# MoE matmuls as pairs in two 64-row tiles, with two score groups and wide evacuations, in a fused attention and MoE kernel

## The chip, the cores and the metric

The kernel runs on one core of one Trainium2 chip. The metric is the device time in microseconds (us), the median of five runs. Engines: PE is TensorE (matmuls; PEld are its weight loads), DVE is VectorE, ACT is ScalarE, POOL is GpSimd, SP is SyncE, which here only issues DMAs. Matmul results land in PSUM: eight banks, each of 128 partitions x 512 float32. A matmul may use the whole array (128 rows of the contraction) or a part of it as a "tile"; two matmuls in the tiles of rows 0-63 and 64-127 can run abreast.

## The reference

```python
# attention with pooled queries: B, H, S, D = 8, 8, 1152, 64; factor 2
q_pool = q.reshape(B, H, S // 2, 2, D).mean(axis=3)          # 576 queries per head
scores = matmul(q_pool, k.T) / sqrt(D)
attn   = softmax(scores)
x      = matmul(attn, v)     # -> (B * 576, H * D) = (4608 tokens, 512)
# MoE layer with a maximum of two branches, d_ff = 1024
h1, h2 = x @ w1, x @ w2
out    = maximum(h1, h2) @ w_out                             # (4608, 512) float32
```

The kernel works in bfloat16 with float32 accumulation. It uses max(h1, h2) = relu(h1 - h2) + h2: with wd = w1 - w2 and w21 = w2 @ w_out, both made once on the chip, out = relu(x @ wd) @ w_out + x @ w21.

## The kernel before

**Work on TensorE.** The 64 heads are taken as 32 pairs. For each pair:

- *Scores* (`scores`, L480-506): keys and pooled queries lie transposed, head 0 in partitions 0-63, head 1 in 64-127. A score group is 512 score columns for both heads: two matmuls abreast in the two 64-row tiles, each into its own bank of a two-bank tensor `sps`. There are 324 groups over the whole run, about 10 per pair. ScalarE then does one exp over both banks (1024 columns), from `sps` into `et`. A group may be overwritten when its exp is done.
- *AV* (`av_jobs`, L399-454): exp(scores) times V with a column of ones for the sum. It comes as two jobs, one per head: three units of nine 128-row matmuls of 65 columns each, and in the first job a unit of 18 column-tiled matmuls for the last 64 queries (the "rest", L427). VectorE then divides into `xnat`.
- *Transposes* bring `xnat` into `xT`, by DMA on SP's queue or, for the first and last batch, by TensorE.

MoE jobs use `xT`. An *h job* (`h_jobs`, L632) makes 128 rows of relu(x @ wd) for up to 512 tokens with four 128-row matmuls; VectorE applies the maximum with zero into the buffer `gT`. A *p job* (`p_job`, L657) makes the output of 128 tokens with twelve 128-row, 512-column matmuls (four with `w21`, eight with `wo`); VectorE copies it into one of four output slots `osb`, from which it is stored. After the last score group ScalarE takes half of these evacuations.

**Banks.** Three score groups take six banks (`sps0` to `sps2`); two banks, `fb0` and `fb1`, are lanes for jobs, one job to a bank. After the last score group the six banks become lanes too (`more_banks`).

**Order.** All instructions are put in order in Python before the program is built. `Plan` keeps for each engine the time at which it is free, with a cost per operation, a latency to other engines and 0.1 us when TensorE changes its tile shape (a unit's `mode`: "f" 128 rows, "s" 64 rows, "c" column tiles). The loop at L991 takes the next piece of TensorE work: a burst of two score groups (three once the attention of a first batch is done) when they can start without a stall, else a unit of a job whose inputs are ready, by rank. On the chip each engine runs its instructions in this fixed order and waits on semaphores. Loads of q, k, v (SP), casts (POOL) and DMA transposes (SP) are put in by due times of the same plan (`flush`, L804).

The lines that carry the order and the lanes:

```python
for g in range(3):                       # more_banks, after the last group
    ...
r = g % 3                                # scores: ring of three groups
...
done = [b for b in range(B) if all(av_half.get(b * NHP + j) == 2 for j in range(NHP))]
return 3 if done else 2                  # burst_size
...
if ready and stall <= 0.1:               # main loop
    emit_burst(ready)
elif fresh:
    emit_unit(min(fresh, key=lambda c: c[1:])[3])
```

Of the kernel before, what the change touches and what calls it, by code (L numbers as in the profile page):

```python
# [15 lines left out]
class Plan:  # L16
# [28 lines left out]

    def when(self, eng, r=(), w=(), after=()):

        if any(k not in self.writer for k in r):
            return 1e9
        t = self.free.get(eng, 0.0)  # L50
        for d in self.deps(r, w, after)[0]:
            p = self.ops[d]
            if p["eng"] != eng or p["dma"] is not None:
                t = max(t, p["seen"] + 0.05)
        return t

    def op(self, eng, fn, r=(), w=(), dma=None, cost=0.1, mode="f", after=(), solo=False):
        n = len(self.ops)
# [6 lines left out]
        self.last[eng] = n  # L65
        t = self.when(eng, r, w, after)
        if dma is not None:
# [5 lines left out]
        else:  # L73
            if eng == "PE" and mode != self.mode:
# [4 lines left out]
        self.ops.append(dict(eng=eng, fn=fn, deps=deps, raw=raw, dma=dma, w=tuple(w),  # L79
                             seen=seen, end=self.free[eng], solo=solo))  # L80
        for k in r:
# [6 lines left out]
    def solve(self):  # L88
# [3 lines left out]
        for n, o in enumerate(ops):  # L92
# [3 lines left out]
            for d in sorted(o["deps"], reverse=True):  # L96
                p = ops[d]
                if p["dma"] is None:
                    if p["eng"] == eng and (eng == "PE" or eng != "DVE" and d not in o["raw"]):
                        continue  # L100
                    key = p["eng"]
                else:
                    key = ("dma", p["dma"])
                if kn.get(key, -1) >= d:
                    continue
                o["waits"].append(d)
                for k, v in p["know"].items():
                    if kn.get(k, -1) < v:
                        kn[k] = v
                kn[key] = max(kn.get(key, -1), d)  # L110
# [39 lines left out]
class Job:  # L150


    def __init__(self, kind, units, evac, done=None, nb=None):
        self.kind, self.units, self.evac, self.done = kind, units, evac, done
        self.nb = nb


def bass_funnel_attn__then__act_maxout2_kernel(
# [32 lines left out]
    with ctx:  # L191
# [33 lines left out]
        gT = g16.rearrange("p (f n) -> p f n", f=NF)  # L225
        osb = [stage[:, NC_ * F + s * E:NC_ * F + (s + 1) * E] for s in range(4)]

        sps = [psum([P, 2, 512], f"sps{g}") for g in range(3)]
        fb = [psum([P, 512], f"fb{g}") for g in range(2)]
        fb += [sps[g][:, half, :] for g in range(3) for half in range(2)]  # L230

# [244 lines left out]
        def skeys(g):  # L476
            return [key for i, t, *_ in pieces(g) for key in (f"kT{i % 3}.{t}", f"qpT{i % 3}")] + (
                ["qpT0.0"] if g == 0 else [])

        def scores(g):  # L480
            r = g % 3

# [133 lines left out]
        ocount = [0]  # L616
        held = {}

        def store(lo, s, c0=0, c1=E, engs=("SP", "SP")):
# [12 lines left out]
        def h_jobs(nb, tail):  # L632
# [4 lines left out]
            for ft in range(NF):  # L637
# [16 lines left out]
                jobs.append(Job("h", [part(ct) for ct in range(NC_)], evac, nb=nb))  # L654
            return jobs

        def p_job(lo, tail, c0=0, c1=E):  # L657
# [75 lines left out]
        X_PE = (0, B - 1)  # L733
        DEPTH = 4.0
        LAG = 600
        Q_PE = 5
# [99 lines left out]

        def more_banks():

            for g in range(3):
                for half in range(2):  # L840
                    m = 2 + 2 * g + half
                    lane[m] = None
                    plan.writer[f"f{m}"] = plan.writer[f"s{g}"]
                    plan.readers[f"f{m}"] = set(plan.readers[f"s{g}"])

        def ready_at(job):
            return plan.when("PE", r=job.units[0][0])

        def burst_size():

            done = [b for b in range(B) if all(av_half.get(b * NHP + j) == 2 for j in range(NHP))]
            return 3 if done else 2

        def more_moe():
            tail = nxt == NGR
            while h_at[0] < len(hblocks):
                n0, n1 = hblocks[h_at[0]]
# [3 lines left out]
                if plan.when("PE", r=keys) > now() + (9.0 if tail else 0.0):  # L861
                    break
                queue["h"].extend(h_jobs(h_at[0], tail))
                h_at[0] += 1
            while p_at[0] + P <= h_end[0] and f"w21{NC_ - 1}" in plan.writer:
                if p_at[0] + P < NTOK:
                    queue["p"].append(p_job(p_at[0], tail))
                else:
                    queue["p"].extend(p_job(p_at[0], tail, *c) for c in ((0, 384), (384, E)))
                p_at[0] += P  # L870

        def refill():

            more_moe()
            soon = now() + (0.05 if nxt else 0.3)
            for kind in "qkxa":
                if queue[kind] and (ready_at(queue[kind][0]) <= soon):
                    return queue[kind].pop(0)
            busy = [j.kind for j in lane.values() if j]
            for kind in "wh" if queue["a"] and "p" in busy else "wph":  # L880
                if queue[kind] and ready_at(queue[kind][0]) <= soon:
                    return queue[kind].pop(0)
            if nxt == NGR:
                for kind in "axph":
                    if queue[kind]:
                        return queue[kind].pop(0)
            return None

        def burst_now(size):
# [11 lines left out]
            for g in todo_g:  # L901
                s = plan.when("PE", r=skeys(g), w=[f"s{g % 3}"])
                stall += max(0.0, s - t)
# [3 lines left out]
        def emit_burst(todo_g):  # L907
# [10 lines left out]
            if nxt == NGR:  # L918
                more_banks()
            if queue["q"]:  # L920
                for kk in (0, 1):
                    if lane[kk] is None and plan.when(
                            "PE", r=queue["q"][0].units[0][0], w=[f"f{kk}"]) <= now() + 0.05:
# [4 lines left out]
        def emit_unit(kk):  # L928
# [5 lines left out]
            job.evac(kk)  # L934
            lane[kk] = None
            if job.kind == "a":
                av_half[job.nb] = av_half.get(job.nb, 0) + 1
# [3 lines left out]
            elif job.kind == "h":  # L941
                h_left[job.nb] = h_left.get(job.nb, NF) - 1
                while h_left.get(h_ok[0]) == 0:
                    h_end[0] = hblocks[h_ok[0]][1]
                    h_ok[0] += 1
            elif job.kind == "p":
                p_parts[job.nb] = p_parts.get(job.nb, 0) + 1
                if p_parts[job.nb] == (2 if job.nb == NTOK else 1):
                    p_got.add(job.nb)
# [41 lines left out]
        while p_end[0] < NTOK:  # L991
            flush()
            for kk in sorted(lane, key=lambda kk: plan.when("PE", w=[f"f{kk}"])):
                if lane[kk] is None:
                    lane[kk] = refill()
            cand = []
            for kk in lane:
                job = lane[kk]
                if job is not None:
                    t = plan.when("PE", r=job.units[0][0], w=[f"f{kk}"])  # L1000
                    cand.append((t, -rank[job.kind], len(job.units), kk))
# [5 lines left out]
            if len(turn) < len(fresh) and plan.mode == "f" and nxt < NGR:  # L1007
                fresh = [c for c in fresh if c not in turn]
            ready, stall = burst_now(burst_size())
            if ready and stall <= 0.1:  # L1010
                emit_burst(ready)
# [72 lines left out]
```

## Time and profile before

| | |
|---|---|
| median of 5 runs | 380.22 us (379.67 to 382.66) |
| the profiled execution | 382.66 us; its span, first to last instruction, 380.9 us |
| granted TensorE clock | 1.0 throughout |
| busy: PE / ACT / POOL / DVE | 357.4 / 316.3 / 161.5 / 149.9 us |
| exps (L493) | 336 instructions, 306.2 us, 1008 ns on average |
| scores (L486) | 1152 matmuls, 100.5 us busy |
| AV (L415, L427) | 2304 + 576 matmuls, 81.9 + 15.2 us |
| h matmuls, 128 x 512 into `fb` (L640) | 192, 380 ns each as recorded |
| p matmuls, 128 x 512 into `fb` (L667) | 195 with `wo` and 96 with `w21`, 380 ns each as recorded |
| evacuation of 128 x 512 (L651, L699) | 692 and 691 ns |
| HBM read / written | 62.91 / 9.44 MB |

How to read it: a matmul's recorded duration runs until its last result is in PSUM, while the next one may already stream; so durations of matmuls overlap, and what one costs is seen from the distance between starts. "Idle before" in a group names what released the first instruction after the idle time. In the chain of work, a piece lasts until the next piece starts. "issue" is time in which the profile shows nothing that the engine waited for.

### The profile page before, as it was taken

To read this page: it belongs to the slowest core of one execution; us is meant where nothing else is said; L and a number is where in the kernel's file an instruction comes from. 1 tells how busy PE (TensorE), PEld (TensorE's weight loads), DVE (VectorE), ACT (ScalarE), POOL (GpSimd) and SP (SyncE) were. 2 spreads that over 40 slices of the span, in tenths; PEclk is the share of its full clock that TensorE was granted. 3 is DMA by queue.
4 is the path that set the end of the run, shared out by engine and by line. 5 is a ranking of instruction groups with operands and counts; after the bars stand their busy time and mean duration, and the time that the engine had idled before them with its cause. 6 is when DMAs were issued, how large, how long until landed. Compare 5 with 4: busy or idle time off the path is not lost.

```text
span 380.9 us, 11393 instructions
## 1 busy us (share of the span) xinstructions
PE 357.4 (94%) x4983; PEld 204.7 (54%) x5040; DVE 149.9 (39%) x348; ACT 316.3 (83%) x358; POOL 161.5 (42%) x133
## 2 busy tenths in 40 slices
PE   2889999999999999999998899999999999999995
PEld 1465555555555555555555355555555555566462
DVE  2565774532344233532253133432343324843121
ACT  1999999999999999999988889998999999103120
POOL 1265996667416750675165318570485120000000
PEclk9999999999999999999999999999999999999999
DMA  7999999999899998998999989997999761012323
GB/s 258 408 393 403 398 236 279 254 261 346 179 201 390 214 243 183 388 245 219 233 338 280 113 239 390 235 281 114 325 268 307 110 209 29 2 29 57 83 65 100
DMA packets 93537, 88.58 MB, mean 233 GB/s; under 512 B 66096, under 2 KB 66352, under 8 KB 93488
## 3 DMA queue, kind: packets, MB, share of 16 engines
q1 hardware_dynamic: 92448, 86.28, 85.8%
q10 hardware_dynamic: 1040, 1.57, 1.1%
q8 instruction: 39, 0.64, 0.7%
q14 instruction: 10, 0.08, 0.1%
HBM read 62.91 MB, written 9.44 MB: 190 GB/s over the span
## 4 chain that ended last, share of the span: by engine, by line
PE 77%; ACT 16%; issue 2%; DMA 2%; DVE 1%; another core or an unknown queue 0%; SPq 0%; ACTq 0%
PE sps L486 18%; PE fb L667 18%; PE fb L415 17%; ACT et L493 16%; PE fb L640 12%; PE sps L667 5%; PE fb L427 3%; PE sps L640 3%; DMA kraw<-in_k_dram 2%; PE fb L606 1%; DVE xnat L447 0%; DVE xnat L442 0%; PE fb L383 0%; PE fb L548 0%
## 5 line engine op out<-in xcount | busy, mean ns | idle before, releaser
L493 ACT ACTIVATE et<-sps 128x1024 bf16<-128x1024 f32 (+1 forms) x336 | 306.2, 1008 | 10.7 <-PE sps L486 8.5
L314 POOL TENSOR_TENSOR qp<-qraw 64x576 bf16<-64x576 f32 x60 | 85.1, 1419 | 54.4 <-DMA qraw<-in_q_dram 47.0
L486 PE MATMUL sps<-qpT,kT 64*128 64x512 bf16 (+7 forms) x1152 | 100.5, 290 | 5.9 <-issue 3.0
L415 PE MATMUL fb<-vE,et 128*128 128x65 bf16 x2304 | 81.9, 193 | 1.2 <-DVE xnat L447 0.5
L415 PEld LDWEIGHTS fb<-vE,et 128*128 128x128 bf16 x2304 | 74.3, 97 | 11.4 <-DVE xnat L447 4.3
L486 PEld LDWEIGHTS sps<-qpT,kT 64*128 64x128 bf16 x1152 | 40.1, 95 | 65.8 <-ACT et L493 33.3
L321 POOL TENSOR_SCALAR vE<-vraw 128x1152 bf16<-128x1152 f32 x32 | 37.8, 1182 | 67.1 <-DMA vraw<-in_v_dram 66.8
L651 DVE TENSOR_SCALAR stage<-fb 128x512 bf16<-128x512 f32 (+3 forms) x62 | 40.1, 646 | 53.9 <-PE fb L640 48.3
L640 PE MATMUL fb<-xT,wd 128*128 128x512 bf16 (+3 forms) x268 | 57.0, 346 | 2.1 <-issue 1.4
L667 PE MATMUL fb<-wo,stage 128*128 128x512 bf16 (+1 forms) x203 | 54.0, 377 | 1.3 <-issue 0.3
L279 POOL TENSOR_SCALAR kbf<-kraw 128x1152 bf16<-128x1152 f32 x31 | 37.5, 1209 | 22.3 <-DMA kraw<-in_k_dram 12.5
L437 DVE RECIPROCAL rc<-fb 128x5 f32<-128x5 f32 (+1 forms) x64 | 12.1, 188 | 83.1 <-PE fb L415 83.0
L640 PEld LDWEIGHTS fb<-xT,wd 128*128 128x128 bf16 x284 | 24.4, 98 | 25.7 <-issue 4.5
L699 DVE COPY stage<-fb 128x512 f32<-128x512 f32 x24 | 16.6, 691 | 43.1 <-PE fb L667 39.3
L667 PEld LDWEIGHTS fb<-wo,stage 128*128 128x128 bf16 x224 | 19.5, 98 | 21.0 <-issue 3.3
L447 DVE TENSOR_TENSOR xnat<-fb,rc 128x256 bf16<-128x256 f32 x64 | 27.2, 425 | 2.2
L667 PE MATMUL fb<-w,xT 128*128 128x512 bf16 (+1 forms) x100 | 26.8, 377 | 0.7 <-issue 0.3
L696 ACT COPY stage<-fb 128x512 f32<-128x512 f32 x3 | 1.8, 586 | 20.3 <-PE fb L667 20.3
L427 PEld LDWEIGHTS fb<-vE,et 128*64 128x64 bf16 x576 | 11.6, 111 | 7.9 <-issue 7.6
L667 PE MATMUL sps<-wo,stage 128*128 128x512 bf16 (+1 forms) x70 | 15.8, 361 | 0.1
L667 PEld LDWEIGHTS fb<-w,xT 128*128 128x128 bf16 x112 | 9.9, 98 | 11.0 <-DVE xnat L447 1.1
L427 PE MATMUL fb<-vE,et 128*64 128x65 bf16 x576 | 15.2, 197 | 0.0
(45 smaller groups left out, 136.6 us busy)
## 6 DMA issues: line engine op xcount, KB each, us to landing
kraw<-in_k_dram SPq DMA_DIRECT2D x32, 576.0 KB, 7.5
vraw<-in_v_dram SPq DMA_DIRECT2D x32, 576.0 KB, 7.6
qraw<-in_q_dram SPq DMA_DIRECT2D x31, 576.0 KB, 7.0
out_dram<-stage SPq DMA_DIRECT2D x59, 128.0 KB, 2.6
xT<-in_moe_w_dram SPq DMA_DIRECT2D x4, 512.0 KB, 10.2
stage<-in_moe_w_out_dram SPq DMA_DIRECT2D x4, 512.0 KB, 13.1
stage<-in_moe_w_dram SPq DMA_DIRECT2D x4, 512.0 KB, 12.9
out_dram<-stage ACTq DMA_DIRECT2D x11, 128.0 KB, 2.6
```

Of the source, the lines that this page charges most:

```text
L279: op("POOL", lambda g: g.tensor_scalar(kbf[s][:, :, :, :].rearrange("p t h d -> p h t d"), kraw[r][:, :, :, :], 1.0, 1.0, ALU.mult, ALU.mu ...
L314: op("POOL", lambda g, half=half, a=a: g.tensor_tensor(qp[s][:, :, half, :], a[:, :, 0, :], a[:, :, 1, :], ALU.add), r=[f"qraw{r}"], w=[f" ...
L321: op("POOL", lambda g: g.tensor_scalar(vE[r][:, :, :, 0:D].rearrange("p t h d -> p h t d"), vraw[r][:, :, :, :], 1.0, 1.0, ALU.mult, ALU.m ...
L415: last = e.matmul(fb[m][:, sb * 66:sb * 66 + 65], et[:, a:a + P], vE[vs][:, t, half, 0:65], start=(t == 0), stop=(t == NT - 1))
L427: last = e.matmul(fb[m][rows(half), NCH * 66:NCH * 66 + 65], et[:, a:a + NB], vE[vs][:, t, half, 0:65], start=(t == 0), stop=(t == NT - 1))
L447: dve(lambda e: e.tensor_tensor(xnat[xs][:, 0:NCH, c:c + D], a[:, 0:NCH, 0:D], rc[half][:, 0:NCH].unsqueeze(2).to_broadcast([P, NCH, D]), ...
L486: last = e.matmul(sps[r][:, h, col:col + hi - lo], kT[i % 3][rows(h), t, :], qpT[i % 3][rows(h), lo:hi], start=True, stop=True)
L493: op("ACT", lambda e: e.activation(et2[:, :, c:c + z - a], sps[r][:, :, a - g * W:z - g * W], EXP, scale=scale), r=[f"s{r}"], w=keys + [f" ...
L640: return e.matmul(fb[m][:, 0:size], wd[:, ct, ft * P:(ft + 1) * P], xT[:, ct, n0:n1], start=(ct == 0), stop=(ct == NC_ - 1))
L651: dve(lambda e: e.tensor_scalar_max(gT[:, ft, g0:g0 + size], fb[m][:, 0:size], 0.0), [f"f{m}"], w, 0.16 + size / 960.0)
L667: return e.matmul(fb[m][:, 0:c1 - c0], lhs, rhs[:, c0:c1], start=(j == 0), stop=(j == NC_ + NF - 1))
L699: dve(lambda e: e.tensor_copy(osb[o][:, :], fb[m][:, :]), [f"f{m}"], [f"osb{o}", f"f{m}"], 0.69)
```

## The change

1. **Duos.** While score groups are left, MoE work comes as pairs of jobs: two h jobs (two blocks of 128 rows of wd's output, same tokens), or two p jobs (two blocks of 128 tokens). Each 128-row contraction is cut into two of 64 rows. In the first half of a duo job, job k = 0 uses array rows 0-63 and job k = 1 rows 64-127; in the second half they swap. Each unit issues two matmuls, one per tile, into the two banks of one two-bank tensor. Their tile shape is that of the scores. At the swap a `fence` makes TensorE wait for its own last matmul on the same banks.
2. **Banks.** When the first MoE work is queued (and the number of groups done is a multiple of three), the score ring goes from three groups to two, and the third pair of banks becomes a pair of lanes. From then on there are two bank pairs for jobs. Two AV halves of one head pair can be joined in one bank pair.
3. **Wide evacuations.** VectorE evacuates both banks of a duo in one instruction of 1024 columns.
4. **Order.** From then on score bursts are of one group, and the main loop has its own rules: it stays with 128-row work until ScalarE's planned lead falls under `FLOOR` (0.1 us) or no score is ready, and goes to 128-row work from a lead of `LEAD` (1.4 us). A duo job starts only when no other lane has a duo with more than `NEAR` (6) units left.

After the last score group everything is as before: what is left of the MoE work is taken as single 128-row jobs on eight lanes.

```diff
+        wide = [psum([P, 2, 512], "fb")] + sps
+        fb = [w[:, half, :] for w in wide for half in range(2)]
...
+        def ring(g):
+            return g % 3 if g < turn_at[0] else (g - turn_at[0]) % 2
         def scores(g):
-            r = g % 3
+            r = ring(g)
...
+        def duo(r, cost, pair, turned):
+            def plan_it(m):
+                op("PE", lambda e: pair(e, m), r=r, w=[f"f{m}", f"f{m + 1}"], cost=cost, mode="s",
+                   fence=turned)
+            return r, plan_it, cost, "s", 2 if turned else 0
...
+        def h_pairs(nb):
...
+                    def pair(e, m):
+                        for k in range(2):
+                            z = rows(turn ^ k)
+                            last = e.matmul(
+                                fb[m + k][:, 0:size], wd[z, ct, (f0 + k) * P:(f0 + k + 1) * P],
+                                xT[z, ct, n0:n1], start=(turn == 0 and ct == 0),
+                                stop=(turn == 1 and ct == NC_ - 1))
+                        return last
+                    return duo([f"wd{ct}"] + xkeys(n0, n1), 0.217 * size / 512, pair, turn == 1 and ct == 0)
+                def evac(m, f0=f0):
...
+                    dve(lambda e: e.tensor_scalar_max(
+                        gT[:, f0:f0 + 2, g0:g0 + size], wide[m // 2][:, :, 0:size], 0.0),
...
+        def p_pair(lo):
...
+                def pair(e, m):
+                    for k in range(2):
+                        z = rows(turn ^ k)
+                        n = lo + k * P
+                        if j < NC_:
+                            lhs, rhs = xT[z, j, n:n + P], w21[z, j, :]
+                        else:
+                            c = n % RING
+                            lhs, rhs = gT[z, j - NC_, c:c + P], wo[z, j - NC_, :]
+                        last = e.matmul(fb[m + k][:, :], lhs, rhs, start=(turn == 0 and j == 0),
+                                        stop=(turn == 1 and j == NC_ + NF - 1))
+                    return last
...
+            def evac(m):
+                ocount[0] += ocount[0] % 2
+                o = ocount[0] % 4
+                ocount[0] += 2
+                for s in (o, o + 1):
+                    if s in held:
+                        store(*held.pop(s))
+                dve(lambda e: e.tensor_copy(
+                    osb2[:, o:o + 2, :], wide[m // 2][:, :, :]), [f"f{m}", f"f{m + 1}"],
...
         def burst_size():
+            if turn_at[0] < NGR:
+                return 1
...
         while p_end[0] < NTOK:
             flush()
+            if phase() == 1 and nxt % 3 == 0 and queue["h"]:
+                turn_at[0] = nxt
+                more_banks((2,))
...
             ready, stall = burst_now(burst_size())
+            if phase() == 2:
+                lead = plan.free.get("ACT", 0.0) - now()
+                soft = [c for c in fresh if lane[c[3]].units[0][3] != "s"]
+                firm = [c for c in fresh if c not in soft]
+                if plan.mode != "s" and soft and (not ready or stall > 0.05 or lead > FLOOR or not CUT):
+                    pick = [c for c in soft if lane[c[3]].units[0][3] == plan.mode] or soft
+                    emit_unit(min(pick, key=lambda c: c[1:])[3])
+                    continue
+                if ready and stall <= (0.005 if firm and lead >= 0.6 else 0.05):
+                    emit_burst(ready)
+                    continue
+                if soft and (lead >= LEAD or not firm or (ready is None and nxt < NGR)):
+                    emit_unit(min(soft, key=lambda c: c[1:])[3])
+                    continue
+                if firm:
+                    emit_unit(min(firm, key=lambda c: c[1:])[3])
+                    continue
```

## The prediction

> **What bounds the kernel now.** I read the page first (busy times, slices, groups), then the sums over stretches of 20 us, then the chain in order of time, then a few microseconds of the timeline. Page, parts 1 and 2:
>
> ```profile
> PE 357.4 (94%) x4983; PEld 204.7 (54%) x5040; DVE 149.9 (39%) x348; ACT 316.3 (83%) x358; POOL 161.5 (42%) x133
> ...
> ACT  1999999999999999999988889998999999103120
> ...
> PEclk9999999999999999999999999999999999999999
> ```
>
> Two engines are full at once: ScalarE until about 325 us, then hardly used; TensorE to the end, at full clock. The stretches (columns: PE, PEld, DVE, ACT, POOL busy, then clock, DMA) split the run into three parts:
>
> ```profile
> 40.00:60.00 20.00, 18.66 (x324) 11.08 (x326) 14.38 (x25) 19.91 (x24) 17.72 (x12) 1.00 1.06 279
> ...
> 80.00:100.00 20.00, 19.71 (x277) 10.60 (x277) 5.05 (x14) 19.74 (x22) 13.99 (x11) 1.00 1.13 285
> ...
> 200.00:220.00 20.00, 16.93 (x206) 9.01 (x209) 5.64 (x13) 17.08 (x20) 9.04 (x7) 1.00 0.98 192
> ...
> 340.00:360.00 20.00, 19.89 (x136) 11.67 (x136) 5.56 (x13) 3.81 (x10) 0.00 (x0) 1.00 0.26 69
> ```
>
> Up to 64.5 us there is no MoE work (start). From 64.5 to 322 us scores, exps, attention-times-V (AV) and MoE share TensorE (joint part). From 322 to 381 us TensorE works off the MoE that is left (tail, 59 us). The chain gives TensorE's prices, since its pieces run on to the start of the next one:
>
> ```profile
> 78.70 2.01 PE fb L415 x63
> ...
> 87.32 0.40 PE fb L427 x18
> 87.73 1.19 PE fb L415 x36
> ...
> 93.04 2.05 PE fb L667 x9
> 95.08 0.86 PE sps L486 x12
> 95.95 2.05 PE fb L667 x9
> ...
> 141.79 1.40 PE fb L667 x6
> ...
> 201.63 1.53 issue
> ...
> 211.00 1.17 issue
> ```
>
> (2.05 - 1.40)/3 = 0.217 us per 128-row, 512-column matmul; what is left of the 1.40 is 0.10 us: the gap before a score burst. The AV pieces say the same: (2.01 - 1.19)/27 = 0.0304 us each, 36 of them 1.09 us, 0.10 left; the column-tiled rest of AV (L427) has 0.30 and 0.10. Score matmuls use 64-row tiles, everything around them 128-row tiles. Over all changes of tile shape in this trace the gap beyond the columns has a median of 92 to 99 ns in either direction; I take **0.097 us per switch**. In the score burst 12 matmuls, two abreast, make three groups: 0.86 - 0.10 = 0.76, so a pair of 64-row, 512-column matmuls costs at most 0.25 us; uninterrupted pairs in the trace start 0.216 us apart (0.010 more where a semaphore wait stands between).
>
> The timeline gives the latencies between TensorE and ScalarE:
>
> ```profile
> 212.18 0.82 PE L486 MATMUL sps<-qpT,kT 64*128 64x128 bf16 x11 [1.17 <-issue]
> ...
> 212.60 2.86 ACT L493 ACTIVATE et<-sps 128x1024 bf16<-128x1024 f32 x3 [1.36 <-PE sps L486]
> ```
>
> From a score group's first matmul to its exp: 0.42. Three exps take 2.86 and one alone 1.04 (its group's mean), so exps follow each other every 0.91. A score matmul that waits for an exp starts 0.05 after its end: 1.09 after that exp's start.
>
> **The change, by its parts.** Where planner and pools decide, I counted in the order of the built program.
>
> *Switches.* A MoE duo is in the scores' tile shape, so only AV, transposes and the weight product still switch. Counted over the whole program: 290 changes of shape before, 202 after (joint part 222 to 130). 88 x 0.097 = **-8.5 us** of TensorE. These lie on the path: counted from the first score group after the first MoE matmul to the last, 264 groups come to 57.5, AV to 64.8, MoE to 105.1 and 222 switches to 21.5, together 248.9 of the 257.5 us, so nothing else covers them. The gain shows in the tail: MoE matmuls issued before the last score rise from 491 full-size units to 524 (a duo counts one), 33 x 0.217 = 7.2 us of tail.
>
> *The duo itself.* No trace shows two row tiles accumulating. Nearest row: score pairs, 0.216 us for 512 columns against 0.217 for one 128-row matmul, so 0 per duo. Bounds: 0 (a stream of 512 columns cannot go below a 512-column stream) and 0.217 (the two run one after the other) on each of 524. I take 0, as the scores have both tiles, both banks and the same weight loads.
>
> The number of weight loads doubles. In score bursts four loads of 93 to 96 ns start within 0.02 us while the first pair streams, and the next pair follows when the first has drained, 136 ns after a 320-column pair: hidden. The Trainium skill, "TensorE: Matmul & The Clock Gate", The mechanism (in Part 3), speaks against this: weight loads overlap running matmuls only when the row group differs, and a duo's next loads go to the same two row groups. By that rule each duo would show a load, some 0.095 us x 524 = +50 us; by the row it is 0.
>
> *The turn.* Half-way the tiles swap banks, and a fence makes TensorE wait for its own last matmul. 55 duo jobs are in the order; 38 carry a wait; in 30 of them at least one other duo or score group (0.217) stands between, in 8 nothing. A 512-column matmul is recorded with 0.38 us and its semaphore is seen 0.04 to 0.05 later: 0.43 - 0.217 = 0.21 us lost, 8 x 0.21 = **+1.7**. Lower end 0 (a later wait would have come anyway), upper 38 x 0.21 = 8.
>
> *Two score groups in place of three.* Now a score may not start until the exp two groups back is done, and everything on TensorE's queue stands behind that wait. One head pair worked by hand from its order (0.217 per group or duo, AV column block of 9 matmuls 0.274, the rest 0.30, switch 0.10). Group c starts at 0, the exps of a, b, c at -1.09, -0.18, 0.73. Then rest and three blocks: group d at 0.217 + 0.30 + 0.82 + 3 x 0.10 = 1.64, its exp 0.42 later at 2.06 (ScalarE, done with c at 1.64, is dry for 0.42). Group e at once, 1.86 (free since 0.73 + 1.09 = 1.82), exp 2.97. Five blocks: group f at 1.86 + 0.217 + 1.37 + 2 x 0.10 = 3.65, exp 4.07 (dry 0.19). One duo: g at 4.08 (free at 4.06), exp 4.98. Four duos: h at 5.17 (free at 5.16). From there windows of three duos and a group, 0.87, against exps every 0.91: TensorE waits 0.04 in each of five. Sum 0.2 us a pair. A pair whose second AV run has six blocks gives 0.24, once, where group e must wait. 26 pairs x 0.21 = 5.5 us. Today's waits: 257.5 - 248.9 = 8.6, less 3.5 for late transposes (the two "issue" pieces and a smaller one), less 2.0 for waits passed in a burst (169 x 0.012), less 1 of small gaps: 2.1. So **+3.4**. Ends: 0 and twice the 5.5, +9.
>
> ScalarE's dry spells cost nothing by themselves, since TensorE is busy in them: exps need 262 x 0.91 = 238 us of a joint part of some 258.
>
> *Waits in the stream.* Groups not preceded by a switch: 169 before, about 211 after, 42 x 0.012 = **+0.5**.
>
> *The turning point.* The ring shrinks at a multiple of three groups, and MoE work starts after 61 groups in place of 59 for the same TensorE work (46.6 us). Where ScalarE sets the pace that is up to 2 x 0.91 less 2 x 0.217 = 1.4 later; 0 where it does not. I take the middle, **+0.7**.
>
> *Wide evacuations, the joined AV halves, stores.* A 512-column evacuation takes 692 ns, 256 columns 422: 0.154 + 1.05 ns per column, so 1.23 us for both banks against 1.38. VectorE (39% busy) covers it. Behind the wide copy on VectorE's queue wait AV's reciprocals, up to 0.54 us later than now; a second bank pair with a duo job covers that. If it is busy too, 0.5 on some of 26 pairs, at most +13 x 0.5 = 6. Four output slots remain and the store queue on SP carries the same transfers (63 out against 61, the two taken from ACT's queue). Loads and transposes keep their number; the late ones at 201 and 211 us I leave where they are: 0, between -3.5 (they fall into cover) and +3.5 (twice as much).
>
> Sum: -8.5 + 1.7 + 3.4 + 0.5 + 0.7 = **-2.2 us**. The profiled execution spans 380.9 and took 382.66; the median of the five is 380.22, 2.4 lower, and I put the difference on the median: **378.0**.
>
> **The rivals.**
> - *Full gain* (waits fall where TensorE is late anyway, as ScalarE drifts by hundredths): -8.5 + 1.7 + 0.5 = -6.3, **373.9**. For: the hand-worked pair is late or just in time at half its groups. Against: the three-duo windows are shorter than an exp.
> - *Slower: two groups are too few.* At the scores next to AV and in the three-duo windows TensorE waits on exps far more than 0.21 a pair. Each 0.1 us a pair is 2.6 us; from 0.37 us a pair it is slower by 0.5%. At 0.6 us: -2.2 + 26 x 0.39 = +8, **388**. For: bursts of one leave no group in hand when a transposed operand comes late, and 1.36 us of ScalarE idle at 211 us happened with three. Against: TensorE, not ScalarE, is the fuller one.
> - *Duos do not overlap fully.* 8 ns each give +4.2 and 382.2; one after the other +114. Against: the score pairs.
> - *Nothing to gain* because transfers set the joint part: DMA is at 0.9 to 1.2 of its engines from 20 to 300 us, and four more output tiles are stored in that time. The tail's 7.2 us come back as late transposes: **380.5**. Against: two holes of about 1.5 us in 257.
>
> **How the numbers follow.** About 0.5%, 1.9 us, is what a measurement can tell from none. Chances: the forecast with its neighbours (376 to 380) 0.33, full gain 0.26, nothing 0.12, two groups too few 0.22, duos not abreast 0.07. The forecast's case lies half on either side of -0.5%; with full gain and a part of it that makes faster 0.47, same 0.22, slower 0.31. The range takes in the full gain (373.9, less 0.9 for covered fences) and the slower case up to 0.5 us a pair: 373 to 386; beyond it lie the rest of that case and serial duos.
>
> **What would show it.** Right: duos 0.216 us apart; about 200 gaps of 0.1 us at changes of tile shape; last score near 325 us and a tail near 52; ScalarE's idle before exps up by 0.4 to 0.6 us a pair, released by scores. Wrong: TensorE idle before scores, released by exps, above 10 us in all; duos 0.23 us or more apart; a longer hole near 200 us; duos waiting on VectorE's wide copies.

## The result, and the profile after

| | before | after |
|---|---|---|
| median of all runs | 381.47 us (95 runs, 378.79 to 385.28) | 379.94 us (53 runs, 378.32 to 383.67) |
| ratio, 95% interval | | 0.9967 [0.9954, 0.9981]: 1.3 us less (0.7 to 1.8) |
| profiled execution, span | 380.9 us | 378.6 us |
| first MoE matmul / end of the last score group | 62.4 / 323.0 us | 64.8 / 328.0 us |
| joint part / tail | 260.6 / 57.9 us | 263.2 / 50.6 us |

The change makes the kernel 0.33% faster; 0.58% was forecast. It is real, and less than the 0.5% that the forecast called a difference. The ratio leaves out runs over 1.5% above the fastest of the same kernel, so it is not the quotient of the two medians. In absolute time the forecast of 378.0 us is 1.9 us off, in part because it was put on a median of five runs (380.22) that lies 1.25 us under the median of all 95.

The page of the kernel after, parts 1, 2 and 4 (busy times, slices, chain):

```profile
PE 359.4 (95%) x5576; PEld 202.5 (53%) x5584; DVE 140.5 (37%) x304; ACT 316.1 (83%) x360; POOL 161.7 (43%) x133
...
ACT  2999999999999999999899999999899999811131
...
PEclk9999999999999999999999999999999999999999
...
PE 67%; ACT 28%; DMA 2%; issue 1%; DVE 1%; SPq 0%
```

Part 4 of the page before:

```profile
PE 77%; ACT 16%; issue 2%; DMA 2%; DVE 1%; another core or an unknown queue 0%; SPq 0%; ACTq 0%
```

The sums of busy time are as before: TensorE full to the end, ScalarE full until about 325 us. What differs is the chain: it runs along ScalarE for 28% of the span, where it did for 16%. Three stretches of 20 us in the joint part and one in the tail (columns: PE, PEld, DVE, ACT, POOL busy, clock, DMA share, GB/s):

```profile
80.00:100.00 20.00, 19.94 (x332) 10.67 (x329) 5.67 (x14) 19.25 (x22) 12.94 (x10) 1.00 1.04 242
180.00:200.00 20.00, 18.93 (x322) 10.70 (x317) 8.13 (x16) 18.60 (x21) 7.22 (x7) 1.00 1.03 221
200.00:220.00 20.00, 19.91 (x341) 10.96 (x337) 5.58 (x14) 18.99 (x22) 11.88 (x10) 1.00 1.07 296
340.00:360.00 20.00, 19.83 (x143) 10.61 (x143) 5.15 (x11) 3.05 (x8) 0.00 (x0) 1.00 0.29 77
```

PE, ACT and the DMA engines are all at 93% or more of the joint part's first and third stretch. In the second, PE lacks 1.07 us: a hole, to which the experiments come back.

**The duos.** The timeline of TensorE at the start of one:

```profile
112.03 1.03 PE L681 MATMUL fb<-xT,wd 64*128 64x512 bf16 x8
112.89 0.38 PE L681 MATMUL sps<-xT,wd 64*128 64x512 bf16 x2
113.11 0.38 PE L492 MATMUL sps<-qpT,kT 64*128 64x512 bf16 x2
113.33 0.81 PE L681 MATMUL sps<-xT,wd 64*128 64x512 bf16 x6
114.02 0.39 PE L492 MATMUL sps<-qpT,kT 64*128 64x64 bf16 x4
```

Eight matmuls are four pairs; the next begins 0.86 us later: 0.215 a pair. A score group fits between at the same pitch (113.11 to 113.33 is 0.22), with no gap for a change of shape.

**What now waits.** Three microseconds further on, the same view:

```profile
114.93 0.39 PE L492 MATMUL sps<-qpT,kT 64*128 64x128 bf16 x4
115.16 0.38 PE L681 MATMUL sps<-xT,wd 64*128 64x512 bf16 x2
115.38 0.59 PE L681 MATMUL fb<-xT,wd 64*128 64x512 bf16 x4
115.85 0.39 PE L492 MATMUL sps<-qpT,kT 64*128 64x192 bf16 x4
116.08 0.59 PE L681 MATMUL fb<-xT,wd 64*128 64x512 bf16 x4
116.77 0.39 PE L492 MATMUL sps<-qpT,kT 64*128 64x256 bf16 x4
116.99 0.81 PE L681 MATMUL fb<-xT,wd 64*128 64x512 bf16 x6
117.68 0.39 PE L492 MATMUL sps<-qpT,kT 64*128 64x320 bf16 x4
```

Score groups start at 114.93, 115.85, 116.77 and 117.68: every 0.91 to 0.92 us, which is the pace of the exps (back to back they start 0.903 us apart). Between the first two stand three units of duo (2 + 4 matmuls), between the second and third only two. Three units and a group are 0.87 us, so the next score waits 0.04; two units leave 0.26.

From the starts of all TensorE instructions in the joint part I worked out how far each stands from the one before beyond the columns that one streams (0.216 us for 512):

| joint part, us | before | after |
|---|---|---|
| changes of tile shape | 223: 21.6 | 130: 12.5 |
| gaps before score matmuls | 8.7, of which 3.5 in three stops (0.49 at 194.0, 1.69 at 203.16, 1.35 at 212.18) | 10.1 |
| gaps from duo to duo and from score to duo (MoE matmuls before) | 0.3 | 3.1 |
| MoE units waiting for transposed x | 0 | 2.4 (1.05 at 183.57, 1.37 at 264.85) |

So the switches fell as forecast, by 9.1 here. The rest of the table took most of that back.

For the two waits on x in the kernel after the profile names no releaser, but a DMA transpose into `xT` lands 0.09 us before each ends (at 183.48 and 264.75). The three stops of the kernel before are something else, although the forecast and the experiments below call them late transposes. No transpose into `kT`, `qpT` or `xT` lands within 0.9 us of their ends. TensorE's three restarts are 254 and 255 recorded instructions apart, and 1.2 to 1.4 us before each ends a 16 KB packet of the queue that the page calls "instruction". There are 39 such packets for TensorE's 10,110 recorded instructions (weight loads and waits included), and 44 for 11,245 in the kernel after. The packet before the first stop came 14.4 us and 442 TensorE instructions behind the one before it. So these stops look like TensorE waiting for its own instructions, whose loads came late; no run tests this by itself.

### The profile page after: what moved, and what is told of

It reads as the page before. It is cut to its first block, busy times and chain, and to the rows that moved or that the text cites. A ratio compares the mean times of both kernels' runs of the same rounds, so it can differ in the third digit from the quotient of the medians.

```text
span 378.6 us, 12481 instructions
## 1 busy us (share of the span) xinstructions
PE 359.4 (95%) x5576; PEld 202.5 (53%) x5584; DVE 140.5 (37%) x304; ACT 316.1 (83%) x360; POOL 161.7 (43%) x133
## 4 chain that ended last, share of the span: by engine, by line
PE 67%; ACT 28%; DMA 2%; issue 1%; DVE 1%; SPq 0%
ACT et L499 28%; PE sps L492 16%; PE fb L418 10%; PE sps L418 8%; PE sps L714 8%; PE sps L749 5%; PE fb L714 5%; PE fb L681 4%; PE sps L681 2%; PE sps L654 2%; DMA kraw<-in_k_dram 2%; PE fb L430 2%; PE fb L654 2%; PE sps L430 1%; PE fb L749 1%
## 5 line engine op out<-in xcount | busy, mean ns | idle before, releaser
L492 PE MATMUL sps<-qpT,kT 64*128 64x512 bf16 (+7 forms) x1152 | 119.1, 291 | 3.9 <-ACT et L499 1.3
L418 PE MATMUL fb<-vE,et 128*128 128x65 bf16 x1368 | 48.6, 193 | 0.5 <-DVE xnat L450 0.5
L418 PEld LDWEIGHTS fb<-vE,et 128*128 128x128 bf16 x1368 | 43.7, 97 | 6.0 <-issue 4.2
L681 PE MATMUL fb<-xT,wd 64*128 64x512 bf16 (+1 forms) x240 | 35.6, 373 | 2.6 <-issue 2.1
L681 PE MATMUL sps<-xT,wd 64*128 64x512 bf16 x224 | 33.0, 376 | 0.1
L418 PE MATMUL sps<-vE,et 128*128 128x65 bf16 x936 | 32.8, 193 | 0.0
L714 PE MATMUL sps<-wo,stage 64*128 64x512 bf16 x224 | 31.7, 376 | 0.0
L418 PEld LDWEIGHTS sps<-vE,et 128*128 128x128 bf16 x936 | 29.7, 97 | 3.4 <-issue 2.9
L714 PE MATMUL fb<-wo,stage 64*128 64x512 bf16 x192 | 27.6, 376 | 0.0
L690 DVE TENSOR_SCALAR stage<-fb 128x1024 bf16<-128x1024 f32 (+1 forms) x15 | 18.1, 1205 | 20.7 <-PE fb L681 20.7
```

Of the source, the lines that this page charges most:

```text
L418: last = e.matmul(fb[m][:, sb * 66:sb * 66 + 65], et[:, a:a + P], vE[vs][:, t, half, 0:65], start=(t == 0), stop=(t == NT - 1))
L492: last = e.matmul(sps[r][:, h, col:col + hi - lo], kT[i % 3][rows(h), t, :], qpT[i % 3][rows(h), lo:hi], start=True, stop=True)
L681: last = e.matmul(fb[m + k][:, 0:size], wd[z, ct, (f0 + k) * P:(f0 + k + 1) * P], xT[z, ct, n0:n1], start=(turn == 0 and ct == 0), stop=(t ...
L690: dve(lambda e: e.tensor_scalar_max(gT[:, f0:f0 + 2, g0:g0 + size], wide[m // 2][:, :, 0:size], 0.0), [f"f{m}", f"f{m + 1}"], w + [f"f{m}" ...
L714: last = e.matmul(fb[m + k][:, :], lhs, rhs, start=(turn == 0 and j == 0), stop=(turn == 1 and j == NC_ + NF - 1))
```

## The experiments

Theory A: TensorE gave up its switches and got waits on exps, through the ring of two groups. Theory B: the gain is lost inside the duos, in fences, banks and the wide copies. After the first four runs a third was formed, theory C: three limits stand close together in the joint part, TensorE's columns and switches, the exps with a ring of two, and the DMA transposes under full DMA load (DMA engines busy all the time); whoever relieves one meets the next. Ratios are to the kernel before on the same chip, with 95% intervals.

**E1 and E2: shorter exps, the order untouched.** From group 60 on an exp over a whole group covers 384 of its 512 columns per head. E1 is made from the kernel after, E2 from the one before.

```diff
+                n = 384 if g >= 60 and z - a == W else z - a
...
-                    et2[:, :, c:c + z - a], sps[r][:, :, a - g * W:z - g * W], EXP, scale=scale),
+                    et2[:, :, c:c + n], sps[r][:, :, a - g * W:a - g * W + n], EXP, scale=scale),
```

> The changed kernel; from group 60 on a full exp covers 384 of the 512 columns per head (the other 128 keep older values, so the output is wrong), and the order is untouched. An exp then takes about 0.82 in place of 1.04 us (row: 128x768, 816 ns). Theory A (the switches saved are paid back in waits on exps, because a score may start only when the exp two groups back is done): the 6.6 us that TensorE waits before scores beyond the semaphore's 10 ns (4.47 + 3.96 less 177 x 0.010) go, 6 us faster than the changed kernel, 0.979 of the kernel before; holes for late transposes may take back 1 to 2. Theory B (the missing gain sits in the duos themselves: fences, swaps, wide copies): no faster than the same cut gives the kernel before, 2 to 3 us.

> The kernel before with the same cut exps, order untouched; the output is wrong in the same way. Theory A: with three groups TensorE waits little on exps: in-burst gaps of 7.8 us, less 3.5 of late transposes and 1.7 of semaphore checks, leave 2.6; so 2 to 3 us faster, 0.993. Theory B: the same gain as in the changed kernel.

Measured: E1 0.9946 [0.9913, 0.9979], 378.5 us; E2 0.9989 [0.9950, 1.0028], 381.0 us. In E1 the gaps before scores fell from 10.1 to some 0.5 us, as theory A says, and yet the kernel gained only some 0.8 us on the changed one. The timeline of E1 (SyncE's queue left out) shows where they went:

```profile
179.95 0.38 PE L715 MATMUL sps<-wo,stage 64*128 64x512 bf16 x2
...
182.72 0.82 PE L682 MATMUL fb<-xT,wd 64*128 64x512 bf16 x6 [2.39 <-DMA xT<-xnat]
...
184.98 1.52 PE L682 MATMUL fb<-xT,wd 64*128 64x512 bf16 x6
```

The first h duo on new tokens waits 2.39 us for a DMA transpose of x. And the same six matmuls that took 0.82 us at 182.72 take 1.52 at 184.98: the clock has gone down (more on this at the end). Beyond the columns streamed, such holes rose from 2.4 us in the kernel after to 5.6 (1.18 at 141.4, 2.56 at 182.7, 1.90 at 263.3). E2 has the same thing in another place, here in its list of waits:

```profile
PE sps L486 <- DMA qpT<-qp: 3.0, 1, 3.0
```

A score waits 3 us for its transposed queries at 284.6, and other holes of 1.42 and 1.12 us stand at 241.8 and 142.9. Theory A names the wait, but not what removing it is worth.

The clock has a part in this, too. The mean granted clock was 0.991 to 0.996 in 11 of the 12 runs of E1 and in 10 of the 12 of E2, against 2 of 54 runs of the kernel after; one spell at half clock like that of E1's profile gives a mean of 0.995 and costs up to 1.7 us. So some of what shorter exps failed to give went to these spells, which in the profiles come with the long holes. The runs at full clock are too few to say how much (E1: one, 377.4 us; E2: two, 377.6 and 378.8).

**E3: the wide evacuation as two narrow ones**, within one place in the order. (The copy of the p duos is split in the same way.)

```diff
-                    dve(lambda e: e.tensor_scalar_max(
-                        gT[:, f0:f0 + 2, g0:g0 + size], wide[m // 2][:, :, 0:size], 0.0),
+                    def two(e):
+                        for k in range(2):
+                            last = e.tensor_scalar_max(
+                                gT[:, f0 + k, g0:g0 + size], fb[m + k][:, 0:size], 0.0)
+                        return last
+                    dve(two,
```

> The changed kernel with two 512-column evacuations (2 x 0.69 us) in place of one of 1024 (1.22 us) for each duo, order untouched. Theory A: VectorE is 37% busy and both bank pairs cover 0.16 us: 0 within 0.5 us against the changed kernel. Theory B: 55 x 0.16 us of later bank release, up to 3 us slower or, if the wide copy was what AV's reciprocals waited for, up to 2 us faster.

Measured: 0.9990 [0.9956, 1.0025], 380.5 us, span 378.9 against 378.6. The gaps before scores are 8.7 us after MoE units against 8.4, those inside the duos the same as in the kernel after. On TensorE the wide form is worth nothing that shows; the ratio differs from the changed kernel's by 0.9 us, inside the intervals.

**E4: hold the h duos back** until 3 us after the planned landing of their transposed x.

```diff
+        HOLD = 3.0
...
+                if not tail and h_at[0] > 0 and max(
+                        plan.ops[plan.writer[key]]["seen"] for key in keys) > now() - HOLD:
+                    break
```

> The changed kernel; the planner queues an h block (after the first) only 3 us after the planned landing of its transposed x. Theory: the two holes of TensorE at 183 and 265 us (1.05 + 1.37 us, a duo waiting for DMA transposes of x) close, since p jobs go first: 2 us faster than the changed kernel, 0.991 of the kernel before. Rival: the transposes for scores (k, q) are then what is late, and nothing is won.

Measured: 0.9998 [0.9964, 1.0032], 381.0 us. Of the h duos' two waits for x one is gone and one is still there (1.37 us at 266.68, after a transpose that landed at 266.59), and a score now waits for its queries as well. Timeline of E4:

```profile
286.45 0.81 PE L714 MATMUL sps<-wo,stage 64*128 64x512 bf16 x6
...
289.60 0.61 PE L492 MATMUL sps<-qpT,kT 64*128 64x256 bf16 x4 [2.33 <-DMA qpT<-qp]
```

Here the hole has moved. All transposes stand in one queue (SP) with the same loads, and postponing one consumer showed the next. This profile is of the slowest of E4's twelve runs (383.9 us, the only one with a mean clock under 0.998), so it shows what can happen, not what does each time. Theory C was formed here.

**E5 to E8: relieve the transfers, the exps, or both, in both kernels.** "Light" means that from the fourth head pair on the loads of k and v bring three of nine column blocks (the output is then not the reference's); "short" is the cut of E1 and E2. The light edit, the same for v:

```diff
+            n = NT if i < 3 else 3
...
-                kraw[s][:, :, :, :].rearrange("p h t d -> p h (t d)"),
-                k[b, h0:h0 + 2, :, :].rearrange("h (p t) d -> p h (t d)", t=NT)),
+                kraw[s][:, :, 0:n, :].rearrange("p h t d -> p h (t d)"),
+                k[b, h0:h0 + 2, :, :].rearrange("h (p t) d -> p h (t d)", t=NT)[:, :, 0:n * D]),
```

> The kernel before, where the loads of k and v from the fourth head pair on bring 3 of 9 column blocks (192 of 576 columns per head; the rest keeps older values, so the output is wrong); order untouched. Theory C (the joint part has three limits close together: TensorE's columns and switches, exps, and late DMA transposes; what one wait loses the next takes): the holes where scores wait for transposes (3.5 us in the profile of the kernel before) close, 3 us faster, 0.992. Theory B (the missing gain of the change sits in the duos: fences, swaps, wide copies): also faster, it says nothing here.

> The changed kernel with the same cut loads. Theory C: the holes of the duos that wait for transposed x (2.5 us) close, the waits on exps (8.4 us before scores) stay: 2.5 us faster than the changed kernel, 0.990 of the kernel before, so again 1 us or less ahead of the other kernel with cut loads. Theory B: the same.

> The kernel before with cut loads and cut exps (384 of 512 columns per head from group 60 on). Theory C: in-burst gaps fall from 7.8 to 1.7 us and no holes take their place: 6 us faster, 0.984. Theory B: the same.

> The changed kernel with cut loads and cut exps. Theory C: both covers gone, the switches show in full: waits on exps (8.4 us) and holes (2.5 us) go, 11 us faster than the changed kernel, 0.968 of the kernel before, and 5 to 6.5 us ahead of the kernel before with both cuts (8.5 for the switches less 1 to 2 for fences and 1 to 2 for the later start). Theory B: it stays 1 to 2 us ahead of that kernel.

Measured, with the earlier runs in the same table (medians in us, ratios to before):

| | before's kernel | after's kernel | what the change is worth |
|---|---|---|---|
| as it is | 1 | 0.9967 | 0.3% |
| short exps (E2, E1) | 0.9989, 381.0 | 0.9946, 378.5 | 0.4% |
| light loads (E5, E6) | 0.9939, 379.2 | 0.9914, 378.4 | 0.25% |
| both (E7, E8) | 0.9834 [0.9791, 0.9877], 375.4 | 0.9679 [0.9639, 0.9718], 369.5 | 1.55%, 5.9 us |

The intervals of the single cuts are 0.3 to 0.4% wide on either side, so 0.3, 0.4 and 0.25% cannot be told apart; the 5.9 us are clear (E7's runs lie between 374.9 and 375.8 us, E8's between 368.7 and 370.1). Nearly the full effect of the switches shows when exps and transfers are both out of the way; relieving either alone gives the change nothing more that shows. That is theory C, with two additions: what is late may be TensorE's instructions as well as transposes, and E1 and E2 also lose time at half clock, which E7 and E8 don't (mean clock 0.998 or more in every run). Theory B falls: E8 has the same fences, banks and wide copies, and gains. The chain of E6 (light loads alone), in a window of 6 us:

```profile
181.40 4.97 ACT et L501 x6
```

and of E8 in the same window:

```profile
180.91 0.65 PE fb L684 x6
181.56 0.22 PE sps L494 x4
181.78 0.65 PE sps L717 x6
182.43 0.22 PE sps L494 x4
```

In E6 the chain is six exps in a row. In E8 it is TensorE alone, duos and score groups end to end: 0.65 and 0.22, so 0.87 a window, with nothing lost. The lists of waits of the joint part say it in one number each; first E6, then E8 (columns: us in total, times, longest; a weight load's idle time lies partly beside streaming matmuls, so 61 us isn't 61 us lost):

```profile
PEld sps L494 <- ACT et L501: 61.0, 165, 0.6
```

```profile
ACT et L502 <- PE sps L494: 37.2, 53, 1.0
...
PEld sps L494 <- ACT et L502: 4.1, 17, 0.5
```

In E6 scores wait for exps. In E8 that row is down to 4.1 us and its reverse is among the first of the list: exps wait for scores.

**E9 and E10: each half of the change alone.** E9 is the kernel before with a ring of two from the first MoE work on and the freed banks as two more lanes; MoE stays in 128-row tiles, score bursts are of two groups.

```diff
+        def ring(g):
+            return g % 3 if g < turn_at[0] else (g - turn_at[0]) % 2
...
-            r = g % 3
+            r = ring(g)
...
+            if turn_at[0] < NGR:
+                return BURST
...
+            if turn_at[0] == NGR and nxt < NGR and nxt % 3 == 0 and queue["h"]:
+                turn_at[0] = nxt
+                more_banks((2,))
```

E10 is the kernel after with the ring kept at three, so duos have one bank pair for all jobs until the last score, and bursts are of two.

```diff
-            return g % 3 if g < turn_at[0] else (g - turn_at[0]) % 2
+            return g % 3
...
-                return 1
+                return 2
...
-                more_banks((2,))
```

> The kernel before with one part of the change alone: from the first MoE work on the score ring has two groups and the freed bank pair gives two more lanes; MoE stays 128-row single jobs, bursts of two groups. In its order 332 changes of tile shape (292 before, all counted the same way) and 551 MoE units before the last score (491). Theory C: a burst of two with a ring of two leaves ScalarE dry about 0.4 us each time (148 bursts), so the joint part grows by 15 to 30 us and the tail shrinks by 60 x 0.217 = 13: 393 to 400 us, 1.035 or more. Rival (two groups cost nothing by themselves, TensorE being the fuller engine): 40 x 0.097 = 4 us slower, 1.01.

> The changed kernel with the ring left at three groups, so duo jobs and joined AV halves have one bank pair alone; bursts of two. 177 changes of tile shape, 424 MoE units before the last score (524). Theory C: with one pair TensorE has nothing to do while VectorE evacuates it (1.2 us and the latencies, some 45 duo jobs and 26 AV pairs); 67 units less than the kernel before are 14.5 us more of tail, and the joint part is no shorter: 393 to 405 us, 1.035 to 1.06. Rival (the third score group is worth more than the second bank pair): no slower than the changed kernel.

Measured: E9 1.0561 [1.0510, 1.0612], 404.1 us; E10 1.0723 [1.0664, 1.0782], 410.2 us. Both lie above the ranges that were expected of them (393 to 400 and 393 to 405 us). E9 spent two spells of 6.83 us at half clock, up to 6.8 us of its time. The waits of E9 in the joint part:

```profile
ACT et L498 <- PE sps L491: 36.2, 82, 4.1
PEld sps L491 <- ACT et L498: 32.8, 71, 1.2
```

and of E10:

```profile
ACT et L499 <- PE sps L492: 25.7, 26, 2.6
PE sps L492 <- ACT et L499: 21.8, 61, 0.9
```

In both, scores wait for exps and exps wait for scores. A burst of two with a ring of two often ends in a wait (E9, gaps before scores some 23 us, and still some 260 switches); with one bank pair, MoE units can't fill the time between scores (E10, some 38 us, and a tail of 72 us). Ring and duos are one change: bursts of one are free only if the work between has the scores' tile shape, and that work is there only with the second bank pair.

**E11 and E12: two duo jobs open at a time, and the kernel after once more.** With 12 for `NEAR` a second duo job may start while the first has up to 12 units left; the aim was a p duo to fill a late h duo's hole.

```diff
-        NEAR = 6
+        NEAR = 12
```

> The changed kernel with NEAR 12 in place of 6: a second duo job starts while the first has up to twelve units left, so a fence or an evacuation finds other work more often. Theory C: fences and waits for banks are at most 2 us, and what they free goes to waits on exps and late transposes: within 1 us of the changed kernel, 0.994 to 0.999. Theory B: 2 to 3 us faster.

> The changed kernel again, on the chip of the runs beside it: 0.9967 as before, between 0.995 and 0.999. In its profile the waits before scores add to 8 to 9 us and the joint part lasts some 263 us; the holes for late transposes are what differs from profile to profile, 1 to 4 us.

Measured: E11 1.0049 [1.0009, 1.0088], 383.6 us: slower, where faster was expected. E12 0.9949 [0.9915, 0.9983], 379.6 us: the result repeated. E11 has larger holes than the kernel after, 2.55 us at 183.25 and 2.07 at 267.9. GpSimd waits 63.1 us for loads of q in its joint part against 38.3 in the kernel after, so the order of transfers moved with the order of TensorE; which of them made it slower I couldn't settle. Five of its twelve runs have a mean clock of 0.994 to 0.996, but the seven others are slow as well (median 382.7 us). None of the variants that compute everything beat the changed kernel by more than the intervals.

## Why the prediction was right or wrong

The step that failed is the wait of scores on exps with two groups. It was sized from one head pair worked by hand, with the waits of today subtracted: +3.9 us with the waits in the stream, where the runs show +5.5. Beside it the gaps between duos and other work, which the forecast left at nothing, came to +1.2. The direction and the mechanism were right.

E5 and E6 have no holes from late transfers, so their difference shows the terms alone. The span of the two profiles falls by 1.4 us (the medians differ by 0.8): the last matmul starts 0.6 us earlier, and what follows it takes 3.5 us in place of 4.3, which the forecast didn't look at (the last matmul is of 128 columns there, not of 512). The terms, all of TensorE:

| term | forecast | E5 to E6 |
|---|---|---|
| switches | -8.5 | -8.6 (292 to 203 changes of shape) |
| the duo itself | 0 | 0: pairs 0.216 us apart |
| fences at the turn | +1.7 | +1.6 (seven of 0.23) |
| other gaps at duos | 0 | +1.2 (0.4 to 1.6) |
| waits before scores (two groups +3.4, stream +0.5) | +3.9 | +5.5 (5.5 to 11.0; two groups +5.3, stream +0.2) |
| AV waiting for a bank | 0 | -0.8 (0.8 to 0) |
| later start | +0.7 | +0.4 (1.9 later, 1.2 of it columns streamed earlier, 0.2 switches) |

*Switches, duo, turn, start:* right, each within 0.3 us. For the duo the forecast had weighed the Trainium skill, "TensorE: Matmul & The Clock Gate", The mechanism (in Part 3), by which weight loads overlap running matmuls only when the row group differs. Here 524 pairs on the same two row groups followed each other at 0.216 us, loads of 94 ns and all: this trace disagrees with that sentence. The same section also lets a load into a background weight buffer go ahead; no run here tells which way these loads took.

*Waits on exps:* the mechanism was right and the size too small, on both sides of the subtraction. Waits of more than 0.02 us before scores are 3.7 us in E5, where the forecast had put today's at 2.1, and 9.0 in E6, where it had 5.5. The hand-worked pair holds: its windows of three duo units cost 0.04 each, 4.6 us in the kernel after. It lacked two things, both in the trace. Eleven windows have two units, not three, and cost 0.26 each, 2.8 us. And where an exp is split in two instructions, the two take 1.17 us from start to start in place of 0.90; the score behind them waits 0.24, four times, 1.0 us. Working one pair by hand and multiplying by 26 took its window for all.

*Other gaps at duos:* a unit that follows a score group stands a little late 187 times, 1.6 us in all. Six gaps of 0.14 to 0.45 us make 1.2 of that; the profile puts them down to VectorE's last step of AV (`xnat`), which frees the bank. Small gaps between MoE matmuls, 0.4 us in all, are gone, and so are seven waits of AV on the same step of VectorE, 0.8 us. The forecast had put the small waits on score groups alone.

*Late transposes, left at 0 between -3.5 and +3.5:* 3.5 us of holes before, 2.4 after. So this difference was small; that was luck, not working, and the forecast had misread the holes before, at whose ends no transpose lands (see the result). Elsewhere with the same loads the holes range from 1.6 us (the second profile of the kernel after, E12) to 5.6 (E1). With light loads there are none, and the runs spread over 1 to 2 us, where they spread over some 6 with full loads: the holes look like most of that spread, together with the half clock that follows the long ones (last section); no run tests this by itself.

*The rivals.* The full gain of 6.3 us needs waits that fall where TensorE is late anyway; that nearly came, and only in E8, where exps and loads were cut (5.9). "Two groups too few" was the right direction, far below its turning point. "Nothing to gain because transfers set the joint part" was half right: light loads alone gave the change nothing (0.25% against 0.33%), so transfers had not eaten its gain, but they do take what shorter exps would give (E1). Forecast marks: the last score came at 327.75 us, not near 325, and the tail was 50.6 us, not 52. All gaps before scores reached 10.1 us, but the mark of 10 that was to show the forecast wrong counted those released by exps, and these are 8.4. ScalarE's waits on scores rose from 7.4 to 12.7 us, 0.2 us a pair and not 0.4 to 0.6. The first MoE matmul before stands at 62.4 us, not at 64.5 as the forecast read it.

The difference missed by 0.9 us (2.2 forecast, 1.3 measured). It came that near by luck: terms too small or not seen, +2.0 together (+1.6 before scores, +1.2 at duos, -0.8 at AV), met an end of the run 0.8 us shorter, which nothing in the forecast foresaw.

## What to carry to other kernels

Where several engines and the DMA queues are at 93% or more in one stretch, price a change by the next limit, not by what it removes: here 8.6 us of TensorE time went away and 1.3 us arrived. Find the next limit by cutting each suspect's work in both kernels, then two at once; with a single cut the change stayed worth 0.25 to 0.4%, with both 1.55%. Look at the granted clock of each run as well, since a cut can open holes that bring it down. And when a buffer ring shrinks, compare each window between two uses with the releasing engine's pace, in the whole order: a window one unit short cost 0.26 us, one just under the pace 0.04.

## What the runs showed of the hardware

I hadn't expected that the clock would matter. In E11 TensorE has a hole of 2.55 us beyond its columns; its timeline:

```profile
180.48 0.38 PE L714 MATMUL sps<-w,xT 64*128 64x512 bf16 x2
...
183.25 1.47 PE L681 MATMUL fb<-xT,wd 64*128 64x512 bf16 x6 [2.38 <-issue]
...
185.33 0.66 PE L714 MATMUL sps<-w,xT 64*128 64x512 bf16 x2
...
186.51 0.82 PE L681 MATMUL fb<-xT,wd 64*128 64x512 bf16 x6
```

Its stretches before, through and after (the last three figures are clock, DMA share, GB/s):

```profile
180.00:183.00 3.00, 0.86 (x12) 0.32 (x8) 0.53 (x2) 2.12 (x3) 0.00 (x0) 1.00 0.35 67
183.00:186.40 3.40, 3.15 (x16) 1.32 (x18) 0.00 (x0) 1.02 (x1) 0.00 (x0) 0.50 0.75 150
186.40:190.00 3.60, 3.60 (x43) 1.75 (x40) 1.23 (x1) 3.24 (x5) 0.00 (x0) 1.00 0.95 217
```

The granted clock is 0.50 for 3.4 us and then 1.00 again; six matmuls take 1.47 us, later 0.82. By the trace's clock record the spell is from 182.99 to 186.40: it starts before the hole ends (a transpose into `xT` lands at 183.16). The same 3.41 us at 0.5 came with the holes of E1 (2.56 us, from 183.89), E2 (3.05 us, from 285.05) and E4 (2.50 us, from 289.53). Holes of 0.5 to 2.07 us left the clock at 1.0, among them those of 1.69 and 1.35 us in the kernel before, 1.05 and 1.37 in the kernel after, 1.90 in E1 and 2.07 in E11. So each of these four holes of 2.5 us or more cost up to 1.7 us on top (half of 3.41). E9 had it without a long hole: while scores waited 0.5 us each time, some 6.8 us from 186.4 were at half clock, and again from 278.6. All six spells start a whole number of 3.413 us steps (49, 79, 80, 49, 50 and 77) after the first entry of the trace's clock record. A stretch of E9:

```profile
188.00:192.00 4.00, 3.69 (x59) 2.64 (x57) 0.00 (x0) 2.35 (x4) 0.00 (x0) 0.50 0.74 134
```

The Trainium skill, "TensorE: Matmul & The Clock Gate", HAM oscillation — how this bites in real kernels (in Part 1), warns of idle gaps longer than about 3.4 us. The four idle times here were shorter, 2.33 to 2.99 us by the timelines, so the trace disagrees with the figure as a safe limit. The window of 3413 ns that the page gives under What's actually happening agrees with the 3.41 us at half clock.

The clock touches the main result a little. Of the 78 runs of the kernel before that stand beside the experiments, 18 have a mean clock of 0.991 to 0.997 (median 384.1 us) and 60 one of 0.998 or more (381.0); of the 54 of the kernel after 52 are at 0.998 or more (380.0). So at full clock the change is worth about 1.0 us by these medians, an estimate, since the runs are of several chips.
